# Splitting x of batch 0 by pair of heads, and the first f pair's products by pair, in an attention and FFN kernel

## The chip, the cores and the metric

The kernel runs on one core of a Trainium2 chip. Its time is the device time in microseconds (us) of one execution. The engines are PE (matrix products; PEld is its loading of weights), DVE (vector), ACT (scalar and activations), POOL (GpSimd) and SP, which issues the transfers. Each engine works through its own queue in order, and semaphores make it wait for results of the others.

## The reference

Eight batches of eight heads, 576 positions, 64 values to a head. Each head gets two attentions, one over positions averaged by fours and repeated, one over a band of seven neighbours; their sum, laid out as 4608 tokens of 512 values, goes through a feed-forward network (FFN) with 2048 hidden values.

```python
out_up = np.repeat(sm_attn(q_d, k_d, v_d), 4, axis=2)      # q_d, k_d, v_d: means over 4 positions
mask = np.abs(pos[:, None] - pos[None, :]) < 4
scores = np.where(mask, scale * np.matmul(q, k.transpose(0, 1, 3, 2)), -1000000000.0)
...
x = np.ascontiguousarray(attn_out.transpose(0, 2, 1, 3)).reshape(B * S, H * D)
h = x @ w_in
r = np.maximum(h, 0.0)
g = s * (r * r) + b
return (g @ w_out).astype(np.float32)
```

w_in and w_out come as 64-bit floats, as pairs of 32-bit words.

## The kernel before

**The work.** A batch's attention is done for four pairs of heads (HP = 4; pair `hp` is heads 2hp and 2hp+1, 128 partitions of values). The result of a batch is `x`, with 128 partitions, four pairs and 576 positions. The FFN goes over 18 blocks of 256 tokens (`t`) and 8 f pairs of 256 hidden values (`p`). Blocks 0 and 1 are the first 512 tokens, all of batch 0; block 2 has its last 64 and the first 192 of batch 1.

**Products of 32-bit accuracy.** x, the hidden values and the weights are each split into a high part, rounded to the fp32r format, and a low part, the difference. Each product is made of three: high by high, low by high, high by low. `split_x` (L517) makes `xh` by a cast on ACT (L530) and `xl` by a subtraction on DVE (L531), for all four pairs of a block at a time. `convert` (L213) turns the 64-bit weights into such halves: ACT L225, DVE L226 to L229, ACT L230 for the high part, POOL L233 for the low one. `split_w(p)` (L235) does this for f pair p.

**The FFN.** `gemm1(t, p)` (L539) makes 24 products of 128x256 into a PSUM bank `ph`: for both halves j of the f pair, for each pair of heads k, the three of L544 to L546. Then ACT applies relu (L554), squares (L555) and casts to `gh` (L556), and DVE makes `gl` (L557). `gemm2(t, p)` multiplies with w_out (L582 to L584) and sums over p; it follows gemm1 two steps later. The order of the steps is a list: blocks 0 and 1 in turn over the first seven f pairs, then block 2, then the rest.

**Batch 0's attention.** `first_unit(0, hp, ...)` (L333) makes one pair: pooled scores (L297) and softmax, the band's scores (L377), softmax (L382 to L390), transposes (L315, L317, L400), copies into block-diagonal form (L403), products with v (L326, L328, L420), and at last two additions on DVE (L423), each of which writes 288 positions of x. POOL adds up v (L282 to L287) and scales the band's weights (L390). Pair 0 has tiles of its own, pairs 1 to 3 borrow memory that later holds weights (`flat` in the trace). Batches 1 and 2 use the same function, their steps spread among the FFN's.

**What sets the order.** A scheduler places each instruction in its engine's queue by priority, in the order of the program unless a block says otherwise, when its own simulation of the kernel finds its inputs ready. Batch 0's pairs stand under `tc.high_priority(offset=400)`, batch 1's under 300; the weights of some f pairs are put back by an offset (BEHIND). In the program the border between attention and FFN is:

```python
        with tc.high_priority(offset=400):
            for _ in first_unit(0, hp, bk):
                pass
    split_w(0)
    load_w(1)
    load_w(2)
    split_x(0)
    split_x(1)
```

Batch 0's attention takes PSUM banks 0 to 3 and 5 to 7 in turn; gemm1 of block 0 uses bank 4, that of block 1 bank 7 (for p below 7). `xh` and `xl` have two buffers each.

Of the kernel before, what the change touches and what calls it, by code (L numbers as in the profile page):

```python
# [10 lines left out]
F32 = mybir.dt.float32  # L11
F32R = mybir.dt.float32r
# [3 lines left out]
ALU = mybir.AluOpType  # L16
AX = mybir.AxisListType

P = 128
B, H, S, D = 8, 8, 576, 64  # L20
HP = H // 2
# [14 lines left out]
TB = 256  # L36
NB = NT // TB
NFP = DFF // 256
NK = DM // P
# [22 lines left out]
def attention_ffn_kernel(ctx, tc, qk, vw_in, vr_in, vdm, qkn, vn, w_in, w_out, s_in, b_in, out):  # L62
    nc = tc.nc
# [4 lines left out]
    two = ctx.enter_context(tc.tile_pool(name="two", bufs=2))  # L68
    ps = ctx.enter_context(tc.tile_pool(name="ps", bufs=1, space=PS))

    def bank(i, shape, name):
        return ps.tile(shape, F32, tag=f"k{i}", name=name)
# [109 lines left out]
    def clear(i):  # L182
        da, vm = room[i]["dg"], room[i]["sc"][:, 1536:1792]
        n = 2 * NG * P
        for j in range(0, n + QV, 488):
            nc.gpsimd.memset(da[:, j : min(j + 488, n + QV)], 0.0)
        nc.gpsimd.memset(vm, 0.0)
        diag[i] = (take(da, 0, [P, 2 * NG, P]), *blocks(da, n, vm))


    wi, wo, wst = {}, {}, {}
# [4 lines left out]
    def load_w(p):  # L196

        parts = (("i", src_i[:, :, 512 * p : 512 * p + 512]), ("o", src_o[:, 2 * p : 2 * p + 2]))
        for op, src in parts:
            st = one.tile([P, 1024, 2], I32, tag=f"w{op}{STAGE[p]}", name="wst")  # L200
            nc.sync.dma_start(st.rearrange("p (k f) t -> p k (f t)", k=src.shape[1]), src)
            wst[(p, op)] = st
# [32 lines left out]
    def split_w(p):  # L235
        with tc.high_priority(offset=-BEHIND.get(p, 0)):
            split_parts(p)

    def split_parts(p):
        wi[p] = one.tile([P, 2, NK, 256], F32R, tag=f"wi{p}", name="wi")  # L240
        wo[p] = one.tile([P, 2, 2, DM], F32R, tag=f"wo{p}", name="wo")
        for op, w in (("i", wi[p]), ("o", wo[p])):
            fl = w.rearrange("p s k f -> p s (k f)")
            if p < len(STAGE):
                st = wst.pop((p, op))
                for j in range(0, 1024, CHUNK[p]):
                    js = slice(j, j + CHUNK[p])
                    convert(st[:, js], fl[:, 0, js], fl[:, 1, js], op, p)
            else:
                for i in range(4):  # L250
                    cs = slice(256 * i, 256 * i + 256)
                    convert(load_quarter(p, op, i), fl[:, 0, cs], fl[:, 1, cs], op, p)


    xt = {}
# [259 lines left out]
    xs = {}  # L515

    def split_x(t):  # L517
        tags = ("os", "xl2") if t == 2 else ("xh", "xl")
        pool = one if t == 2 else two
        xh = pool.tile([P, HP, TB], F32R, tag=tags[0], name="xh")  # L520
        xl = pool.tile([P, HP, TB], F32R, tag=tags[1], name="xl")
        t0 = t * TB
        while t0 < (t + 1) * TB:
            b = t0 // S
            while (b, HP - 1) not in complete:
                next(gen)
            n = min((t + 1) * TB, (b + 1) * S) - t0
            src = xt[b][:, :, t0 - b * S : t0 - b * S + n]
            dst = slice(t0 - t * TB, t0 - t * TB + n)
            nc.scalar.copy(xh[:, :, dst], src)  # L530
            nc.vector.tensor_tensor(  # L531
                xl[:, :, dst], src, xh[:, :, dst].bitcast(F32), ALU.subtract)
            t0 += n
        xs[t] = (xh, xl)

    gt = {}
    oacc = {}

    def gemm1(t, p):  # L539
        xh, xl = xs[t]  # L540
        ph = bank(6 if t >= 3 and p % 2 else 7 if t == 1 and p < HF else 4, [P, 2, TB], "ph")
        for j, k in itertools.product(range(2), range(NK)):
            f = slice(P * j, P * j + P)
            nc.tensor.matmul(ph[:, j], wi[p][:, 0, k, f], xh[:, k], start=(k == 0), stop=False)  # L544
            nc.tensor.matmul(ph[:, j], wi[p][:, 0, k, f], xl[:, k], start=False, stop=False)  # L545
            nc.tensor.matmul(ph[:, j], wi[p][:, 1, k, f], xh[:, k], start=False, stop=(k == NK - 1))  # L546
        if t >= 3 and p % 3 == 2:
            both = one.tile([P, 2, 2, TB], F32R, tag="xl2", name="gb")
            gh, gl = both[:, 0], both[:, 1]
        else:  # L550
            gh = two.tile([P, 2, TB], F32R, tag="gh", name="gh")
            gl = two.tile([P, 2, TB], F32R, tag="gl", name="gl")
        with tc.high_priority():
            nc.scalar.activation(ph, ph, AF.Relu)  # L554
            nc.scalar.activation(ph, ph, AF.Square)  # L555
            nc.scalar.copy(gh, ph)  # L556
            nc.vector.tensor_tensor(gl, ph, gh.bitcast(F32), ALU.subtract)  # L557
        gt[(t, p)] = (gh, gl)
# [47 lines left out]
    def load_ahead(i):  # L606
        for j in range(i, min(i + 3, EU)):
            load_pair(*units[j])
# [11 lines left out]
    for hp in range(HP):  # L620
        load_ahead(hp)
        if hp > 1:
            clear(hp)
        with tc.high_priority(offset=400):
            for _ in first_unit(0, hp, bk):
                pass
    split_w(0)
    load_w(1)
    load_w(2)
    split_x(0)  # L630
    split_x(1)


    order = [(t, p) for p in range(HF) for t in range(2)]
# [37 lines left out]
    for st, (t, p) in enumerate(order):  # L672
        gemm1(t, p)
        if st in at_step:
            split_w(at_step[st])
            if at_step[st] + 2 < len(STAGE):
                load_w(at_step[st] + 2)
        advance(st + 0.5)
        pend.append((t, p))
        if len(pend) > (2 if t < 3 else 3):  # L680
            gemm2(*pend.pop(0))
        advance(st + 1)
        if (t, p) in splits:
            split_x(splits[t, p])
# [64 lines left out]
```

## Time and profile before

| what | value |
|---|---|
| three runs | 993.43, 995.52, 996.3 us; median 995.52 |
| profiled execution, its own time | 995.95 us |
| its span | 994.2 us |
| PE busy | 957.1 us (96%) |
| PEld busy | 853.8 us |
| DVE, ACT, POOL busy | 620.4, 476.6, 467.1 us |
| mean granted clock of PE | 0.976 |

Busy time is the time in which an engine has an instruction running. The granted clock is the share of PE's full speed. A row of a time line gives start and length in us, the engine, the line of the code, the operation, and the tiles as output<-inputs; neighbouring rows of one line are drawn together with their count, and a bracket at the end gives the idle time before the row and what ended it. PE's rows overlap, so the distance of two starts is what a product takes of PE's time.

### The profile page before, as it was taken

What the parts mean: (1) busy time and instruction counts of PE and PEld (TensorE: products, weight loads), DVE (VectorE), ACT (ScalarE), POOL (GpSimd) and SP (SyncE); (2) the same over time, 40 slices, a digit from 0 to 9 for tenths busy, and PEclk for the clock granted to TensorE, in tenths of its full rate; (3) what the DMA queues carried; (4) which work ended last, traced back from release to release, by engine and by line L of the source; (5) the groups of instructions that cost most, each with busy time, mean ns of one, the idle gap of its engine ahead of it and who ended that gap; (6) DMA issues with size and microseconds to landing.
All of it is one profiled execution on the core that took longest, in us unless ns stands there. A gap on an engine that the chain in (4) does not pass through costs nothing.

```text
span 994.2 us, 18568 instructions
## 1 busy us (share of the span) xinstructions
PE 957.1 (96%) x7346; PEld 853.8 (86%) x7346; DVE 620.4 (62%) x1108; ACT 476.6 (48%) x1141; POOL 467.1 (47%) x491
## 2 busy tenths in 40 slices
PE   5769899999999999999999999999999999999998
PEld 4558788788898989898999899989898999999997
DVE  5899985322447688877778887586878772211111
ACT  4867675433465444443456344454546453333231
POOL 9544552000027668676676777474777660000000
PEclk9659999999999999999999999999999999999999
DMA  9728413111231323231333133131323110000000
GB/s 313 251 79 274 137 40 96 36 50 33 88 117 62 114 79 121 87 101 63 97 100 134 64 103 100 37 134 45 128 72 122 63 42 1 23 1 22 1 22 22
DMA packets 32103, 86.27 MB, mean 87 GB/s; under 512 B 3344, under 2 KB 7952, under 8 KB 32016
## 3 DMA queue, kind: packets, MB, share of 16 engines
q1 hardware_dynamic: 32016, 85.08, 26.0%
q8 instruction: 58, 0.95, 0.4%
q14 instruction: 29, 0.24, 0.1%
HBM read 75.63 MB, written 9.44 MB: 86 GB/s over the span
## 4 chain that ended last, share of the span: by engine, by line
PE 71%; DVE 9%; DMA 8%; POOL 5%; ACT 4%; issue 3%; SPq 1%; DVEq 0%; POOLq 0%; ACTq 0%
PE ph L544 11%; PE ph L546 11%; PE ph L545 11%; PE po L582 11%; PE po L583 10%; PE po L584 10%; DMA wst<-in_moe_w_out_dram 3%; DMA tqk<-in_qk_dram 2%; POOL pr L455 2%; PE sa L297 2%; PE up L328 1%; DVE es L229 1%; DVE es L228 1%; DMA wst<-in_moe_w_in_dram 1%; POOL acc L477 1%
## 5 line engine op out<-in xcount | busy, mean ns | idle before, releaser
L544 PE MATMUL ph<-xh,wi 128*128 128x256 f32 x1152 | 328.4, 285 | 2.8 <-ACT xh L530 2.1
L545 PE MATMUL ph<-xl,wi 128*128 128x256 f32 x1152 | 325.4, 283 | 3.4 <-DVE xl L531 3.4
L546 PE MATMUL ph<-xh,wi 128*128 128x256 f32 x1152 | 325.9, 283 | 0.0
L455 POOL TENSOR_TENSOR pr<-lqk 128x576 f32<-128x576 f32 x140 | 202.3, 1467 | 87.9 <-DMA lqk<-in_qkn_dram 71.7
L544 PEld LDWEIGHTS ph<-xh,wi 128*128 128x128 f32 x1152 | 218.4, 190 | 9.7 <-ACT xh L530 2.4
L545 PEld LDWEIGHTS ph<-xl,wi 128*128 128x128 f32 x1152 | 218.4, 190 | 8.5 <-DVE xl L531 3.7
L546 PEld LDWEIGHTS ph<-xh,wi 128*128 128x128 f32 x1152 | 218.8, 190 | 0.8
L554 ACT ACTIVATE ph<-ph 128x512 f32<-128x512 f32 x144 | 83.7, 581 | 248.4 <-PE ph L546 248.3
L582 PE MATMUL po<-wo,gh 128*128 128x512 f32 x456 | 183.8, 403 | 3.1 <-ACT gh L556 2.9
L583 PE MATMUL po<-wo,gh 128*128 128x512 f32 x456 | 182.9, 401 | 0.0
L584 PE MATMUL po<-wo,gl 128*128 128x512 f32 x456 | 180.2, 401 | 0.0
L557 DVE TENSOR_TENSOR gl<-ph,gh 128x512 fp32r<-128x512 f32 x114 | 78.1, 685 | 129.5 <-ACT gh L556 127.5
L477 POOL TENSOR_TENSOR acc<-acc,pv 128x576 f32<-128x576 f32 x80 | 115.2, 1440 | 67.4 <-DVE acc L477 38.3
L457 DVE TENSOR_REDUCE st<-pr 128x9 f32<-128x576 f32 x140 | 106.0, 757 | 42.6 <-POOL pr L455 40.2
L582 PEld LDWEIGHTS po<-wo,gh 128*128 128x128 f32 x456 | 86.2, 189 | 19.3 <-ACT gh L556 4.2
L584 PEld LDWEIGHTS po<-wo,gl 128*128 128x128 f32 x456 | 86.4, 190 | 17.5
L583 PEld LDWEIGHTS po<-wo,gh 128*128 128x128 f32 x456 | 86.4, 189 | 15.9
L556 ACT CAST gh<-ph 128x512 fp32r<-128x512 f32 x114 | 66.6, 584 | 65.2 <-PE po L583 64.0
L476 DVE TENSOR_TENSOR pv<-lv,st 128x576 f32<-128x576 f32 x120 | 87.4, 748 | 16.8 <-POOL acc L477 16.2
L555 ACT ACTIVATE ph<-ph 128x512 f32<-128x512 f32 x144 | 83.7, 582 | 3.2
L287 POOL TENSOR_TENSOR dq<-vq 64x64 f32<-64x64 f32 x58 | 21.7, 373 | 112.8 <-PE up L326 110.6
L583 PE MATMUL po<-wo,gb 128*128 128x512 f32 x120 | 48.0, 400 | 0.0
(143 smaller groups left out, 1294.9 us busy)
## 6 DMA issues: line engine op xcount, KB each, us to landing
tqk<-in_qk_dram SPq DMA_DIRECT2D x30, 584.0 KB, 3.9
lqk<-in_qkn_dram SPq DMA_DIRECT2D x20, 768.0 KB, 4.2
lv<-in_vn_dram SPq DMA_DIRECT2D x20, 480.0 KB, 3.6
out_dram<-os SPq DMA_DIRECT2D x17, 512.0 KB, 3.1
wst<-in_moe_w_in_dram SPq DMA_DIRECT2D x7, 1024.0 KB, 7.9
wst<-in_moe_w_out_dram SPq DMA_DIRECT2D x7, 1024.0 KB, 5.3
tvd<-in_vdm_dram SPq DMA_DIRECT2D x29, 160.0 KB, 2.9
tvr<-in_vr_dram SPq DMA_DIRECT2D x29, 128.0 KB, 2.1
```

The costliest lines, as they stand in the source:

```text
L455: nc.gpsimd.tensor_tensor(pr, lqk[:, 0:CH], lqk[:, CH + o : 2 * CH + o], ALU.mult)
L457: nc.vector.tensor_reduce(ls[:, :, o], pr, AX.X, ALU.add)
L476: nc.vector.tensor_tensor(pv, lv[:, o : o + CH], w, ALU.mult)
L477: (nc.vector if o % 3 == 1 else nc.gpsimd).tensor_tensor(acc[:, :, h], acc[:, :, h], pv, ALU.add)
L544: nc.tensor.matmul(ph[:, j], wi[p][:, 0, k, f], xh[:, k], start=(k == 0), stop=False)
L545: nc.tensor.matmul(ph[:, j], wi[p][:, 0, k, f], xl[:, k], start=False, stop=False)
L546: nc.tensor.matmul(ph[:, j], wi[p][:, 1, k, f], xh[:, k], start=False, stop=(k == NK - 1))
L554: nc.scalar.activation(ph, ph, AF.Relu)
L555: nc.scalar.activation(ph, ph, AF.Square)
L582: nc.tensor.matmul(po[m], gh[:, j, ms], wo[p][:, 0, j], start=first, stop=False)
L583: nc.tensor.matmul(po[m], gh[:, j, ms], wo[p][:, 1, j], start=False, stop=False)
L584: nc.tensor.matmul(po[m], gl[:, j, ms], wo[p][:, 0, j], start=False, stop=last)
```

## The change

A new function `split_pair(t, hp)` splits one pair of heads of one block: a cast of 128x256 on ACT and a subtraction of 128x256 on DVE. It makes the block's two tiles when it is first called for that block. It is called for blocks 0 and 1 right behind each pair of batch 0, at that pair's priority; the calls of `split_x(0)` and `split_x(1)` behind the weights are taken away. In `gemm1(0, 0)` and `gemm1(1, 0)` the 24 products are put in the order of the pairs of heads (all of pair 0 for both halves j, then pair 1 and so on), as one accumulation over the bank: the first product starts it and the last one ends it. All other steps keep their order. The whole diff:

```diff
@@ -533,17 +533,34 @@
             t0 += n
         xs[t] = (xh, xl)
 
+    def split_pair(t, hp):
+
+        if t not in xs:
+            xs[t] = tuple(
+                two.tile([P, HP, TB], F32R, tag=tag, name=tag) for tag in ("xh", "xl"))
+        xh, xl = xs[t]
+        src = xt[0][:, hp, TB * t : TB * t + TB]
+        nc.scalar.copy(xh[:, hp], src)
+        nc.vector.tensor_tensor(xl[:, hp], src, xh[:, hp].bitcast(F32), ALU.subtract)
+
     gt = {}
     oacc = {}
 
     def gemm1(t, p):
         xh, xl = xs[t]
         ph = bank(6 if t >= 3 and p % 2 else 7 if t == 1 and p < HF else 4, [P, 2, TB], "ph")
-        for j, k in itertools.product(range(2), range(NK)):
+
+        jks = list(itertools.product(range(2), range(NK)))
+        apart = t < 2 and p == 0
+        if apart:
+            jks.sort(key=lambda jk: jk[1])
+        for i, (j, k) in enumerate(jks):
             f = slice(P * j, P * j + P)
-            nc.tensor.matmul(ph[:, j], wi[p][:, 0, k, f], xh[:, k], start=(k == 0), stop=False)
+            first = i == 0 if apart else k == 0
+            last = i == len(jks) - 1 if apart else k == NK - 1
+            nc.tensor.matmul(ph[:, j], wi[p][:, 0, k, f], xh[:, k], start=first, stop=False)
             nc.tensor.matmul(ph[:, j], wi[p][:, 0, k, f], xl[:, k], start=False, stop=False)
-            nc.tensor.matmul(ph[:, j], wi[p][:, 1, k, f], xh[:, k], start=False, stop=(k == NK - 1))
+            nc.tensor.matmul(ph[:, j], wi[p][:, 1, k, f], xh[:, k], start=False, stop=last)
         if t >= 3 and p % 3 == 2:
             both = one.tile([P, 2, 2, TB], F32R, tag="xl2", name="gb")
             gh, gl = both[:, 0], both[:, 1]
@@ -624,11 +641,11 @@
         with tc.high_priority(offset=400):
             for _ in first_unit(0, hp, bk):
                 pass
+            for t in range(2):
+                split_pair(t, hp)
     split_w(0)
     load_w(1)
     load_w(2)
-    split_x(0)
-    split_x(1)
 
 
     order = [(t, p) for p in range(HF) for t in range(2)]
```

## The prediction

> **What bounds the kernel now.** I read the page's head first, then a table of stretches, then PE's waits, then the time lines of DVE, GpSimd (POOL) and PE around the place that the change touches. The profiled execution took 995.95 us by its own time, of which the span is
>
> ```profile
> span 994.2 us, 18568 instructions
> ```
>
> so about 1.8 us lie around it. The median of the three runs is 995.52 us, 0.43 below. My sums are made on 995.95 and carried over to the median. The table of stretches gives, for each, its length, then the busy time of PE, PEld, DVE, ACT and POOL, the granted clock and the DMA share.
>
> ```profile
> 30.00:58.00 28.00, 21.03 (x340) 16.50 (x331) 23.23 (x58) 22.81 (x64) 11.76 (x12) 0.58 0.53 174
> 40.00:43.10 3.10, 0.00 (x0) 0.00 (x0) 3.10 (x11) 1.99 (x5) 1.04 (x1) 0.50 0.01 5
> 45.00:50.00 5.00, 5.00 (x82) 4.33 (x79) 4.28 (x11) 4.92 (x15) 0.89 (x1) 0.50 0.42 173
> 52.00:60.00 8.00, 5.53 (x37) 4.07 (x38) 6.31 (x16) 6.30 (x16) 2.36 (x2) 0.50 0.37 101
> 62.00:68.00 6.00, 0.58 (x1) 0.28 (x1) 6.00 (x6) 3.74 (x6) 5.85 (x9) 0.50 0.12 33
> 76.00:100.00 24.00, 23.35 (x254) 20.40 (x251) 22.99 (x38) 18.98 (x39) 11.86 (x9) 1.00 0.81 274
> 100.00:125.00 25.00, 21.88 (x230) 18.40 (x229) 23.05 (x35) 17.40 (x39) 13.88 (x12) 0.93 0.42 137
> 125.00:200.00 75.00, 72.52 (x632) 61.81 (x631) 43.03 (x86) 42.10 (x101) 22.32 (x27) 0.97 0.18 57
> ```
>
> Three things are to be seen. From 125 us on PE is busy nearly all the time (72.52 of 75), so what counts there is only when PE gets there. From 62 to 68 us PE stands nearly still (0.58 of 6.00) while DVE is full (6.00 of 6.00): this is the border between attention and the FFN, where the change lies. And from 76 to 125 us DVE is nearly full as well (22.99 of 24, then 23.05 of 25), with PE losing 3.1 us in the second of these: DVE is close behind PE there. What PE waited for from 62 to 200 us:
>
> ```profile
> PE ph L545 <- DVE xl L531: 3.4, 1, 3.4
> PE po L582 <- ACT gh L556: 2.4, 2, 2.0
> PE ph L544 <- ACT xh L530: 2.1, 1, 2.1
> PE tp L315 <- ACT pd L308: 1.6, 1, 1.6
> PE sl L372 <- ACT pd L301: 0.7, 1, 0.7
> ```
>
> The longest wait and the third are those of the first FFN products for the two splits of batch 0's x: 5.5 us together. The fourth and fifth are products of batch 1's attention that wait for the chain over DVE and ACT; the fourth is this one:
>
> ```profile
> 118.47 0.89 PE L315 MATMUL tp<-ident,pd 96*80 96x96 f32 x3 [1.65 <-ACT pd L308]
> ```
>
> Why the split takes so long is shown by DVE's time line (start, length, engine, line):
>
> ```profile
> 62.53 0.39 DVE L423 TENSOR_TENSOR x<-ol,flat 128x288 f32<-128x288 f32 x1
> 62.84 0.75 DVE L229 SCALAR_TENSOR_TENSOR es<-wst,es 128x512 int32<-128x512 int32 x1
> 63.51 4.47 DVE L531 TENSOR_TENSOR xl<-x,xh 128x1024 fp32r<-128x1024 f32 x1
> ...
> 69.84 1.21 DVE L531 TENSOR_TENSOR xl<-x,xh 128x1024 fp32r<-128x1024 f32 x1
> ```
>
> The two L531 are the same operation on the same shape, once 4.47 us and once 1.21. Beside the long one POOL ran without a hole:
>
> ```profile
> 63.12 0.65 POOL L286 TENSOR_TENSOR dq<-vt 80x64 f32<-80x64 f32 x1
> 63.73 1.26 POOL L233 TENSOR_TENSOR wo<-es,wo 128x512 fp32r<-128x512 f32 x1
> 64.95 0.45 POOL L283 TENSOR_TENSOR vq<-tvr 128x128 f32<-128x128 f32 x1
> 65.36 0.31 POOL L286 TENSOR_TENSOR dq<-vt 80x64 f32<-80x64 f32 x1
> 65.64 1.25 POOL L233 TENSOR_TENSOR wi<-es,wi 128x512 fp32r<-128x512 f32 x1
> 66.86 1.70 POOL L282 TENSOR_TENSOR vt<-tvd 80x256 f32<-80x256 f32 x1
> ```
>
> I read 4.47 - 1.21 = 3.26 us as time in which DVE was kept out by POOL. Last, PE's products of the first f pair:
>
> ```profile
> 68.42 0.41 PE L546 MATMUL ph<-xh,wi 128*128 128x256 f32 x1
> 68.63 0.41 PE L544 MATMUL ph<-xh,wi 128*128 128x256 f32 x1
> ...
> 72.97 0.28 PE L544 MATMUL ph<-xh,wi 128*128 128x256 f32 x1
> 73.09 0.28 PE L545 MATMUL ph<-xl,wi 128*128 128x256 f32 x1
> ...
> 75.32 0.28 PE L546 MATMUL ph<-xh,wi 128*128 128x256 f32 x1
> ...
> 78.58 0.39 PE L544 MATMUL ph<-xh,wi 128*128 128x256 f32 x1 [0.65 <-DVE gl L557]
> ```
>
> They start 0.21 us apart at first and 0.12 us apart once the clock is up; the 48 of both blocks end at 75.60. At 78.58 the second f pair begins.
>
> **The change part by part.** What the splits cost as they are and in pieces shows in the answers for lines 530 and 531 up to 160 us (shortest, median, longest in ns; the shortest is in both cases the one of 256 elements, in the split of block 2):
>
> ```profile
> L530 ACT CAST xh<-x x3: 398/1040/1046, 60.3 to 140.3; 128x1024 fp32r<-128x1024 f32 x2, 128x256 fp32r<-128x256 f32 x1
> L531 DVE TENSOR_TENSOR xl<-x,xh x3: 953/1214/4471, 63.5 to 142.7; 128x1024 fp32r<-128x1024 f32 x2, 128x256 fp32r<-128x256 f32 x1
> ```
>
> Removed: two casts of 128x1024 on ACT (2.09 us) and two subtractions on DVE (4.47 + 1.21 = 5.68 us), all between 60.3 and 71.1 us. Added: eight casts of 128x256, 8 x 0.40 = 3.2 us, and eight subtractions. A free piece is worth a quarter of the free 1.21, some 0.3, and I take 0.35 with its overhead; the one that was measured took 0.95. Upper bound for a blocked one: 0.35 + 3.26 = 3.6 us. No instruction moves on the SP or POOL queue and no DMA is issued by a split; the splits pass the conversion of pair 0's weights in the order of the program, and take the attention's own priority.
>
> *DVE's term.* Two of the eight pieces must follow the last pair of heads, six go ahead of it. The stretch behind the last pair loses 5.68 us and gets two pieces; POOL's train lies there, so I take the 0.95 row for each: 5.7 - 1.9 = 3.8 us. Ends: 5.7 - 0.7 = 5.0 if both are free, and 5.7 - 7.2 = -1.5 if both are blocked in full, which leaves room for a loss.
>
> *The six earlier pieces* lie between 30 and 58 us: 6 x 0.35 = 2.1 us on DVE and 6 x 0.40 = 2.4 us on ACT, in a stretch in which DVE is idle for 28 - 23.23 = 4.8 us and ACT for 28 - 22.81 = 5.2. That idle time is their cover, twice what they need; where it doesn't lie at the right place they push the last pair back, by 4.5 us at most. I take 1.0. DVE's lead behind the border is then 3.8 - 1.0 = 2.8 us.
>
> *PE's term.* The new order (by pair of heads, both halves of f) lets 36 of the 48 products run before the last pair is there. It adds none, and one product costs the same. They need the first f pair's weights, whose last low part is done at 31.86 + 2.52 = 34.4 us:
>
> ```profile
> 31.86 2.52 POOL L233 TENSOR_TENSOR wi<-es,wi 128x512 fp32r<-128x512 f32 x2
> ```
>
> PE has holes: 3.10 us at 40 to 43.1 us and 8.00 - 5.53 = 2.5 us at 52 to 60. In the first only block 0's products of the first pair will be ready for sure (6); the second takes 2.5 / 0.21, some 11. So 17 are gone by 60 us and 31 are left. With the 1.0 of delay they start at 63.0: the first 4 us at 0.21 are 19 products, the other 12 at 0.12 take 1.4: end at 68.4, against 75.6. PE's lead is 7.2 us. The last x is there before (62.92 + 1.0 + 0.40 + 0.95 = 65.3), so that wait is hidden by the products of the other pairs; if POOL's train holds the last piece up to 66.86 + 1.0, by 0.5 us it isn't.
>
> *What ends last.* PE's lead can be kept only as far as DVE and the weights follow. The weights do: the tightest is the sixth f pair, whose low part is done at 129.98 and whose first product starts at 138.69, 8.7 us later.
>
> ```profile
> 128.37 1.61 POOL L233 TENSOR_TENSOR wi<-es,wi 128x512 fp32r<-128x512 f32 x1 [4.43 <-ACT wi L230]
> ```
>
> ```profile
> 138.69 0.28 PE L544 MATMUL ph<-xh,wi 128*128 128x256 f32 x1
> ```
>
> DVE does in part: its weight conversions can be put off within that slack, but the attention chain of batch 1, at which PE already waits before 118.47 us, can't. So the gain lies between DVE's lead of 2.8 and PE's of 7.2; I take the middle, 5.0 us. 995.95 - 5.0 = 991.0 for the profiled execution, 990.5 for the median.
>
> *Two rules weighed against rows.* Row: L531 began at 63.51 while L286 was running (to 63.77), and ended at 67.98; four further POOL operations began before that, two of them L233 at their full 1.25 us. The Trainium skill, "SBUF — State Buffer", section "Who interferes with whom", says that whichever of DVE and GpSimd issues first holds the shared ports for the whole instruction and that the other blocks until it is finished. By that rule L531 would have ended near 63.77 + 1.21 = 65.0; the row is 3.0 us later, so the trace disagrees about how long the loser waits. By the rule a piece waits for one POOL operation at most (1.26), two cost at most 3.2 us, and DVE's lead is at worst 5.7 - 3.2 - 1.0 = 1.5 us.
>
> Row: from 45 to 50 us PE is busy for 5.00 of 5.00 us at a clock of 0.50. The Trainium skill, "TensorE: Matmul & The Clock Gate", section "Part 1: The HAM clock gate (the "warmup" mystery)", has the clock raised after about 3.4 us of sustained activity. The trace disagrees for these small attention products (the FFN products' own rise, 68.0 to about 72.5, fits). By the rule the 19 slow products would be 0.09 us shorter, PE's lead 8.9 and the time 989.7 instead of 990.5.
>
> **The rivals.** *All of PE's lead arrives.* The conversions give way within their slack of 8.7 us and the attention's waits move with the order of PE's queue. For it: DVE is idle for 32 of 75 us from 125 us on, so it can catch up. Against: 23.05 of 25 busy before that. 995.5 - 7.2, with some cold products fewer: 987.5, down to 985.
>
> *The lead is swallowed.* PE comes earlier and waits longer for batch 1's chain and for gl, and the clock falls in these waits (0.93 on the mean of 100 to 125 us already shows this once). For it: that DVE row. Then the gain is 0 to 2.8 us: 994.
>
> *It doesn't happen.* Priorities order the queues; the products may stay behind the attention's in PE's queue, or wait for whole tiles. Against the second: xh at 60.3 started before x's last part was written at 62.53, so parts are waited for by themselves. Then DVE's few microseconds are lost in the earlier pieces: 995.
>
> *Slower: early products block PE's queue.* PE works in order. A product of an early pair stands ahead of attention products of the later pairs, and waits for its xl piece; behind it wait L297, L377 and L420, and behind them DVE and ACT, which need those results. If such a piece meets POOL as L531 did, all lose 3.26 us (pair 0's pieces fall near the two L233 at 31.86). From three such waits it decides: 5.0 - 3 x 3.26 = -4.8, so 1000.3. Against: before 60 us POOL is idle for more than half of the time (11.76 of 28). By the skill's rule on the ports such a wait is 1.26 at most, and this rival would hardly be there; as the row speaks against the rule, I leave it its chance.
>
> **How the numbers follow.** A measurement of this kernel tells about 0.3%, 3 us, from no change. Forecast 0.44 (990.5, its own range 987.5 to 993), all of PE's lead 0.18 (987.5), swallowed 0.20 (994), doesn't happen 0.08 (995), slower 0.10 (1000.3). Faster by over 0.3% is the first two, 0.62; within 0.3% the next two, 0.28; slower 0.10. The range goes from 985 to 997.5: it leaves out the slower case (0.10) and the outermost ends of the others (together under 0.10).
>
> **What would show each step.** Right: eight L530 and L531 pieces near 0.40 and 0.35 to 0.95 us; some 17 FFN products before 60 us; the wait for L531 gone or under 1 us; the 48 products done near 68 us; the second f pair near 71; a longer wait of PE on attention (L372, L315) at 100 to 125 us, by 2 us or so. Wrong: x of the last pair more than 2 us later than 62.9; pieces of 2 us and more; PE waits on L531 before 60 us; the second f pair no earlier than 77; or a lead that is there at 125 us and gone by 200.

## The result, and the profile after

The changed kernel takes 1001.01 us (median of 6 runs, 999.64 to 1002.17) beside 995.44 us for the kernel before (6 runs, 993.43 to 997.21). The ratio is 1.0051, with a 95% interval of 1.0036 to 1.0066: slower by some 5 us. The forecast of 990.5 us had the wrong sign, and its range ended at 997.5. The profiled execution took 1000.06 us by its own time, 4.1 us more than that of before. The head of its page:

```profile
span 998.3 us, 18577 instructions
PE 955.2 (96%) x7346; PEld 851.8 (85%) x7346; DVE 627.8 (63%) x1114; ACT 479.0 (48%) x1147; POOL 467.6 (47%) x491
```

The table of stretches of the changed kernel, with the columns of the prediction's:

```profile
62.00:68.00 6.00, 2.91 (x8) 1.98 (x8) 6.00 (x8) 3.37 (x7) 4.92 (x9) 0.50 0.10 35
76.00:100.00 24.00, 23.53 (x242) 21.02 (x243) 22.50 (x33) 16.38 (x35) 11.15 (x7) 0.88 0.74 271
100.00:125.00 25.00, 23.23 (x216) 20.49 (x215) 23.00 (x33) 16.38 (x30) 15.54 (x13) 1.00 0.37 113
125.00:200.00 75.00, 69.36 (x669) 59.27 (x669) 44.89 (x93) 45.18 (x114) 21.84 (x31) 0.95 0.23 68
250.00:560.00 310.00, 306.80 (x2206) 276.01 (x2205) 227.75 (x397) 150.83 (x379) 191.23 (x185) 1.00 0.30 96
```

The last of these stretches in the kernel before:

```profile
250.00:560.00 310.00, 309.74 (x2239) 280.89 (x2237) 227.18 (x399) 150.87 (x381) 193.63 (x186) 1.00 0.29 96
```

The border (62 to 68 us) did improve: PE is busy for 2.91 us where it had 0.58. From 125 to 200 us PE loses 3.2 us against before. And from 250 to 560 us, nearly 180 us behind the last instruction that the diff touches, PE does 309.74 - 306.80 = 2.9 us less work at the same clock of 1.00. That last loss was in no step of the prediction. What PE waited for there (waits of PE, 250 to 560 us, changed kernel: total us, times, longest):

```profile
PE ph L561 <- DVE gl L574: 1.8, 3, 1.4
PE ph L561 <- DVE gb L574: 1.0, 1, 1.0
```

In the kernel before PE waits for neither in that stretch. The longest of these waits, in the time line of the changed kernel:

```profile
520.00 0.97 POOL L283 TENSOR_TENSOR vq<-tvr 128x128 f32<-128x128 f32 x1
520.57 3.55 DVE L531 TENSOR_TENSOR xl<-x,xh 128x1024 fp32r<-128x1024 f32 x1
520.93 0.73 POOL L282 TENSOR_TENSOR vt<-tvd 80x256 f32<-80x256 f32 x1
521.62 1.42 POOL L477 TENSOR_TENSOR acc<-acc,pv 128x576 f32<-128x576 f32 x1
524.04 0.68 DVE L574 TENSOR_TENSOR gl<-ph,gh 128x512 fp32r<-128x512 f32 x1
...
524.77 0.39 PE L561 MATMUL ph<-xh,wi 128*128 128x256 f32 x1 [1.37 <-DVE gl L574]
```

A later block's split stands ahead of gl in DVE's queue and meets POOL, 3.55 us where the prediction's free row has 1.21; gl is late, and PE stands for 1.37 us. The kernel before has the same split ahead of the same gl:

```profile
516.56 0.74 POOL L282 TENSOR_TENSOR vt<-tvd 80x256 f32<-80x256 f32 x1
517.84 1.21 DVE L531 TENSOR_TENSOR xl<-x,xh 128x1024 fp32r<-128x1024 f32 x1
518.06 2.29 POOL L477 TENSOR_TENSOR acc<-acc,pv 128x576 f32<-128x576 f32 x1 [0.76 <-DVE acc L477]
518.97 0.68 DVE L557 TENSOR_TENSOR gl<-ph,gh 128x512 fp32r<-128x512 f32 x1
```

So it is not the place of the split in the queue that differs here, but what POOL does when it starts. Before, POOL stands still then (L282 was over 0.54 us earlier); its next operation, L477, starts 0.22 us behind the split and is the one that takes longer (2.29 us, 1.42 in the rows above). With the change L283 is still running when the split starts, and the split ends behind three POOL operations. Ahead of this place the queues do differ. In the traces they are those of before again from 463 us on; up to there neighbours are exchanged (behind 250 us mostly gl, gb or a reduction a few places earlier or later on DVE, one operation on POOL, three transfers on SP). The scheduler orders every queue by its own simulation, so a changed beginning can move ties long behind it. How these exchanges add up to the shift at 520 us was not followed step by step.

### The profile page after: what moved, and what is told of

Read it like the earlier page. It is cut to its first block, busy times and chain, and to the rows that moved or that the text cites. A ratio compares the mean times of both kernels' runs of the same rounds, so it can differ in the third digit from the quotient of the medians.

```text
span 998.3 us, 18577 instructions
## 1 busy us (share of the span) xinstructions
PE 955.2 (96%) x7346; PEld 851.8 (85%) x7346; DVE 627.8 (63%) x1114; ACT 479.0 (48%) x1147; POOL 467.6 (47%) x491
## 4 chain that ended last, share of the span: by engine, by line
PE 61%; DVE 13%; POOL 12%; DMA 7%; issue 5%; ACT 3%; SPq 0%; POOLq 0%; DVEq 0%; ACTq 0%
PE ph L561 9%; PE ph L562 9%; PE ph L563 9%; PE po L599 9%; PE po L600 9%; PE po L601 9%; POOL pr L455 4%; POOL acc L477 3%; DMA lqk<-in_qkn_dram 2%; DMA tqk<-in_qk_dram 2%; DVE es L228 1%; DVE es L229 1%; DMA wst<-in_moe_w_out_dram 1%; PE sa L297 1%; DVE st L457 1%
## 5 line engine op out<-in xcount | busy, mean ns | idle before, releaser
L477 POOL TENSOR_TENSOR acc<-acc,pv 128x576 f32<-128x576 f32 x80 | 114.5, 1431 | 67.8 <-DVE acc L477 36.8
```

The costliest lines, as they stand in the source:

```text
L477: (nc.vector if o % 3 == 1 else nc.gpsimd).tensor_tensor(acc[:, :, h], acc[:, :, h], pv, ALU.add)
```

## The experiments

Two theories stood at first. T1: the border costs next to nothing, and the loss lies in the later order of the queues. T2: the loss is made at the border (late x of the last pair, late chain of batch 1), and what follows only carries it. All ratios are to the kernel before, with the 95% interval; the kernel before had 995.58 to 995.96 us beside them.

**A barrier ahead of the step (4, 0)**, in both kernels, is reached at about 305 us and lets all engines start from there together.

```diff
     for st, (t, p) in enumerate(order):
+        if (t, p) == (4, 0):
+            tc.strict_bb_all_engine_barrier()
         gemm1(t, p)
```

> The kernel before with a barrier of all engines ahead of step (4, 0), near 305 us, so that the queues behind it stand in one order whatever went before. Both theories expect it a few us above 995.4, say 998 to 1006, for emptying and refilling the engines; it is only the base for the next run.

> The changed kernel with the same barrier; behind it the queues are in the same order as in bar_before. Theory 1 (the border between attention and FFN gains some 3 us that is used up by 210 us, and the 4 to 5 us are lost between 210 and 560 us, where the queues' order differs far from the change): within 1.5 us of bar_before. Theory 2 (all is lost at the border, by the later last pair and the low clock): 4 to 6 us above bar_before.

Measured: 1005.52 us (1.0096, 1.0082 to 1.0111) without the change and 1006.14 (1.0109, 1.0095 to 1.0122) with it. The barrier itself costs 10 us; with it on both sides the change costs 0.6 us, inside the intervals. That speaks for T1: what is done up to 305 us can be had with the changed border at about the same time. In both, the split near 520 us takes 1.22 us.

**One part alone.** order_only keeps the old splits and only orders the first products; pieces_only splits by pair and keeps the old order of the products.

```diff
-            for t in range(2):
-                split_pair(t, hp)
...
+    split_x(0)
+    split_x(1)
```

> The whole-block splits as before, only the first f pair's products by pair of heads. Both theories: the products wait for the whole split, nothing changes, 995.4 within 1.5 us.

```diff
-        apart = t < 2 and p == 0
+        apart = False
```

> The splits in pieces as in the change, the first f pair's products in the old order. Theory 1: the queues fall back into the order of the kernel before by some 250 us, so no later loss; the border alone decides, and with 9 instead of 18 products of each block free of the last pair it gains little or nothing: 994 to 998. Theory 2: the last pair is as late as in the change and fewer products are done ahead, 18 x 0.12 to 0.21 us more: 1003 to 1005.

Measured: 995.38 us (0.9999, 0.9986 to 1.0011) and 998.64 us (1.0032, 1.0017 to 1.0047). The queues of order_only are those of before, line by line: without pieces no product can start earlier, and its ratio shows how well no change is measured. The pieces alone cost 3.2 us, although pieces_only has the queues of before from 240 us on and no PE idle time from 250 to 560 us. So something can be lost at the beginning too.

**The same border, another later order.** Batch 2's attention stands under a priority of 60. With 50 the changed kernel keeps its own order up to 199 us and has that of the kernel before from 240 us on; the kernel before, with 50, keeps its own order up to 181 us and has that of the changed kernel from 250 us on.

```diff
-            with tc.high_priority(offset=300 if done < NY[1] else 60 if done < NY[1] + NY[2] else 0):
+            with tc.high_priority(offset=300 if done < NY[1] else 50 if done < NY[1] + NY[2] else 0):
```

> The changed kernel with the priority of batch 2's attention lowered by a hair (offset 50 for 60). By the program as it is built, all queues stand as in the changed kernel up to about 200 us, and from about 230 us on as in the kernel before: the change's border with the old later order. Theory 1 (the loss is in the later order): 994 to 997.5. Theory 2 (the loss is at the border): 1000 to 1002.

> The kernel before with the same hair (offset 50 for 60). Its queues stand as before up to about 200 us and from about 240 us on as in the changed kernel: the old border with the later order of the change. Theory 1: slower than the kernel before by 3 to 5 us, 998.5 to 1000.5. Theory 2: within 1.5 us of 995.5.

Measured: after_offset50 995.17 us (0.9996, 0.9985 to 1.0008); before_offset50 994.0 us (0.998, 0.997 to 0.9991). The first refutes T2: the whole change at the border, and no loss. Since it shares all queues with the changed kernel up to 199 us, the 0.55% between the two are made behind that. The second refutes T1 in its simple form, that the later order is bad by itself: the kernel before gains 2 us with it.

**When and where the pieces are made.** late_pieces leaves only those of the last pair at the attention's priority and puts the others behind pair 0's weights in the program (in the trace, three of those six xl pieces still start by 54 us); pool_pieces makes the subtractions on POOL; last_first orders the first products from the last pair backwards, so that no product is early.

```diff
-            for t in range(2):
-                split_pair(t, hp)
+            if hp == HP - 1:
+                for t in range(2):
+                    split_pair(t, hp)
     split_w(0)
+    for hp in range(HP - 1):
+        for t in range(2):
+            split_pair(t, hp)
```

> As the change, but the pieces of pairs 0 to 2 at the natural priority behind pair 0's weights; only the last pair's pieces keep the attention's priority. From about 220 us on its queues stand as in the kernel before. If the pieces on DVE and ACT push the last pair back (by 3.2 us in the change), its x comes within 1 us of 62.9 again and the first f pair's products end at 69 to 71: 993 to 996. Rival, that the early products in PE's queue push it back: x stays near 65.7, 996 to 998.

```diff
-        nc.vector.tensor_tensor(xl[:, hp], src, xh[:, hp].bitcast(F32), ALU.subtract)
+        nc.gpsimd.tensor_tensor(xl[:, hp], src, xh[:, hp].bitcast(F32), ALU.subtract)
```

> As the change, but the eight xl pieces are made by GpSimd instead of DVE. From about 210 us on its queues stand as in the kernel before. If DVE's queue is what holds the pieces and the last pair back, the last pair's x comes at 63 to 64.5, the last xl piece within 2 us of it instead of 3, and the time is 993 to 996. Rival, that GpSimd's own train of operations holds the last piece: last xl piece at 68 or later, 996 to 998.

```diff
-            jks.sort(key=lambda jk: jk[1])
+            jks.sort(key=lambda jk: -jk[1])
```

> The eight pieces as in the change, but the first f pair's products in the opposite order, the last pair of heads first, so that no product can run ahead of it. From about 220 us on the queues stand as in the kernel before. If the pieces themselves (on DVE and ACT) make the last pair late, its x comes at 65 to 66 as in the change. If the early products in PE's queue do it, its x comes at 62.5 to 63.5. Time: 997 to 1000 in the first case, 995 to 997 in the second; there are no early products to gain from in either.

Measured: 996.19 us (1.0002, 0.9985 to 1.0019), 997.59 us (1.0025, 1.0013 to 1.0037) and 994.99 us (0.9994, 0.9981 to 1.0007). All three have the later order of before. Without early products, and with the pieces, last_first is even with the kernel before, as after_offset50 is with all of them: early products bring nothing. pieces_only, with the same pieces and 18 early products, is 3.8 us slower than last_first by the ratios; why is not shown. Taking the subtractions from DVE (pool_pieces) doesn't help: 0.25% slower. The last pair's x (the start of the second L423) is at 64.98 us in late_pieces and at 65.24 in pool_pieces, and pool_pieces has its last xl piece at 69.32, so both times the rival holds; in last_first x is at 63.96, between the two cases.

**Fewer pieces, and the priority once more.** three_and_one splits three pairs at once behind the third and the last pair alone; three_and_one_o50 has the priority of 50 as well; after_offset100 is the changed kernel with 100 for the 60.

```diff
-            for t in range(2):
-                split_pair(t, hp)
+            if hp >= HP - 2:
+                for t in range(2):
+                    split_pairs(t, 0 if hp == HP - 2 else hp, hp + 1)
```

> As the change, but pairs 0 to 2 split at once (128x768, one cast and one subtraction a block) when pair 2 is done, then the last pair: four of each operation instead of eight, none in the stretch of GpSimd's first weight lows. From about 210 us on the queues stand as in the kernel before. If single pieces held by GpSimd and their number make the last pair late, its x comes within 1.5 us of 62.9 and the time is 993 to 995.5. If any work put there does, x is at 65 again and the time 996 to 998.

> three_and_one with offset 50 for 60: its queues fall into the changed kernel's later order from about 240 us on. If that later order is bad by itself, 3 to 5 us above three_and_one. If it is only bad with the change's border, whose batch 1 is late (x of batch 1 at 172.5 against 164), it is 1 to 3 us below three_and_one, as before_offset50 was below the kernel before.

```diff
-            with tc.high_priority(offset=300 if done < NY[1] else 60 if done < NY[1] + NY[2] else 0):
+            with tc.high_priority(offset=300 if done < NY[1] else 100 if done < NY[1] + NY[2] else 0):
```

> The changed kernel with offset 100 for 60: all queues as in the changed kernel but for a handful of swaps between about 160 and 240 us, then the changed kernel's later order to the end. In three runs that later order showed 2 to 4 us of PE waiting for gl and gb between 250 and 560 us, with the other order at most 0.3. If that is the change's loss, these waits are here again and the time is 998 to 1001. If the loss hung on chances of the stretch around 200 us, which is swapped here, the time is 994 to 997 with the waits there or not.

Measured: 1001.5 us (1.0052, 1.004 to 1.0064), 999.09 us (1.0032, 1.002 to 1.0044) and 997.24 us (1.0014, 1.0001 to 1.0027). three_and_one is as slow as the change, with the later order of before; its time is lost ahead of that order. Its last x is at 65.31 us, the case "any work put there", but its time lies 3.5 us above that case. The two others have the later order of the changed kernel: three_and_one_o50 is 2.4 us below three_and_one, the second of its cases, and after_offset100 has the waits again but stays below the 998 us that they were to bring.

**What the runs add up to.** Call the later order of the kernel before A, that of the changed kernel B. PE's waits from 250 to 560 us in the three other kernels with B are before_offset50:

```profile
PE ph L544 <- DVE gl L557: 1.4, 1, 1.4
PE ph L544 <- DVE gb L557: 0.6, 1, 0.6
```

after_offset100:

```profile
PE ph L561 <- DVE gl L574: 2.0, 3, 1.5
PE ph L561 <- DVE gb L574: 0.6, 1, 0.6
```

and three_and_one_o50:

```profile
PE ph L561 <- DVE gl L574: 2.5, 3, 1.3
PE ph L561 <- DVE gb L574: 1.4, 1, 1.4
```

after_offset50 and three_and_one, both with A, have none. The split near 520 us takes 3.55 us in all four kernels with B, where POOL's L283 runs when it starts, and 1.21 or 1.22 us in the ten others, where POOL stands still then. In the table, "at the end" is the ratio less 1 times 995.5 us. "250 to 560" is PE's idle time there, from the profile, less the 0.26 us of before; the clock is 1.00 there in all of them, and from 560 us on PE is busy in each but for at most 0.2 us until the last 4 us of the program. The last column is the difference of the two: what must have come by 250 us. "At the end" carries some 1.0 to 1.5 us of uncertainty, and "by 250 us" at least as much, as its other term is one execution's.

| kernel | border | later order | at the end | 250 to 560 | by 250 us |
|---|---|---|---|---|---|
| changed kernel | pieces by pair | B | +5.1 | +2.9 | +2.2 |
| after_offset50 | pieces by pair | A | -0.4 | -0.3 | -0.1 |
| after_offset100 | pieces by pair | B | +1.4 | +2.5 | -1.1 |
| before_offset50 | as before | B | -2.0 | +1.8 | -3.8 |
| three_and_one | three and one | A | +5.2 | -0.3 | +5.5 |
| three_and_one_o50 | three and one | B | +3.2 | +3.9 | -0.7 |

Two things are shown. B costs 1.8 to 3.9 us between 250 and 560 us, in all four kernels that have it, by waits for gl and gb; A costs nothing there. And the changed border is neutral when A follows it (-0.4 us, and 0.6 with the barriers). A third is read off with less certainty: with two of the borders B is 3.8 us (-3.8 to the 0 of the kernel before) and 6.2 us (+5.5 to -0.7) better by 250 us, which more than pays for the waits behind; with the changed border it isn't, at 60 (+2.3 against A), and is within the uncertainty at 100 (-1.0). So the change loses 2.9 us to the waits of B. The 2.2 us ahead of them are less sure: the two profiled executions are 4.1 us apart, which leaves 1.2. And the stretch up to 250 us isn't alike in two executions: the granted clock from 125 to 250 us is 0.97 in the changed kernel and 1.00 in bar_after, though the two have the same queues up to 281 us, and 0.03 of 125 us are nearly 4 us. What makes the stretch from 176 to 247 us, where the queues with 60 and with 100 differ, go worse with 60 stays open.

The fastest kernel of all leaves the border alone: before_offset50, one number changed, 994.0 us.

## Why the prediction was wrong

**The step that failed is "What ends last".** It took the gain to lie between DVE's lead of 2.8 and PE's of 7.2 us, and 5.0 in the middle. At the border the runs showed no gain in place of the 5.0 us (after_offset50, -0.4 us with 1.2 of uncertainty either way). DVE's lead was nil. PE's was 2.1 us at the second f pair, and while step (0, 4) still started 3.0 us earlier than before (122.04 for 125.08), step (2, 0), which needs batch 1's x, started 8.3 us later (175.88 for 167.56): the prediction's sign "a lead that is there at 125 us and gone by 200". And the order of the queues, which the prediction took as fixed behind the border ("No instruction moves on the SP or POOL queue"), changed up to 463 us; on POOL the L233 of wo now stands at 63.73 us ahead of the L286 that it followed.

**The six earlier pieces: 1.0 us of delay taken, 3.2 measured.** The additions that write x (the view of line 423, 57 to 175 us: count, shortest, median and longest in ns, first and last start), before:

```profile
L423 DVE TENSOR_TENSOR x<-ol,ups x8: 441/444/452, 79.5 to 164.2; 128x288 f32<-128x288 f32 x8
L423 DVE TENSOR_TENSOR x<-ol,flat x2: 390/420/451, 59.6 to 62.5; 128x288 f32<-128x288 f32 x2
```

and with the change:

```profile
L423 DVE TENSOR_TENSOR x<-ol,ups x8: 442/448/453, 84.2 to 172.9; 128x288 f32<-128x288 f32 x8
L423 DVE TENSOR_TENSOR x<-ol,flat x2: 445/446/447, 62.8 to 65.7; 128x288 f32<-128x288 f32 x2
```

The last pair's x (second row of each) is 65.7 - 62.5 = 3.2 us later, which the prediction had named as a sign of being wrong (over 2). In last_first, with the pieces and no early products, the same two start at 60.75 and 63.96, 1.2 and 1.4 us later. The clock of the attention doesn't explain this: four kernels with the queues of before have this x at 62.5 to 63.0 us, while their clock from 0 to 62 us goes from 0.78 to 0.94. By this one pair of kernels about 1.3 us are the pieces' and 1.8 the early products', which stand in PE's queue ahead of the last pairs' attention. The sum isn't that simple, though: with 18 early products pieces_only has its x at 63.79 and late_pieces at 64.98. Early products in the way are the mechanism of the rival "slower", at some 1.8 us instead of three times 3.26; it alone didn't make the kernel slower, as after_offset50 shows.

**DVE's term: 2.8 us taken, nothing measured.** The pieces have the size that was taken:

```profile
L544 DVE TENSOR_TENSOR xl<-x,xh 128x256 fp32r<-128x256 f32 x8 | 4.6, 579 | 0.0
```

Eight of them take 4.6 us in place of 5.68. What failed is where the last two stand. DVE's time line of the changed kernel:

```profile
62.83 0.45 DVE L423 TENSOR_TENSOR x<-ol,flat 128x288 f32<-128x288 f32 x1
63.19 0.54 DVE L387 TENSOR_REDUCE sm<-pl 128x12 f32<-128x384 f32 x1
63.65 0.68 DVE L229 SCALAR_TENSOR_TENSOR es<-wst,es 128x512 int32<-128x512 int32 x1
64.25 1.49 DVE L227 TENSOR_SCALAR es<-es 128x512 int32<-128x512 int32 x1
65.66 0.45 DVE L423 TENSOR_TENSOR x<-ol,flat 128x288 f32<-128x288 f32 x1
66.03 2.09 DVE L226 TENSOR_SCALAR es<-es 128x512 f32<-128x512 f32 x1
68.03 0.69 DVE L388 TENSOR_SCALAR sm<-sm 128x12 f32<-128x12 f32 x1
68.64 0.41 DVE L544 TENSOR_TENSOR xl<-x,xh 128x256 fp32r<-128x256 f32 x1
...
70.05 0.36 DVE L544 TENSOR_TENSOR xl<-x,xh 128x256 fp32r<-128x256 f32 x1
```

The weights' conversions (L226 to L229) and the softmax of the next pair (L387, L388) stand in the gap that the pieces were to leave. The piece of block 0 starts at 68.64, though its x was there at 63.28 and its cast at 63.7, and the old xl of block 0 was done at 67.98: the blocking by POOL went over to L227 (1.49) and L226 (2.09). The same two operations on the same shape take 0.41 and 0.42 at 69.58 and 70.92 us, so 1.08 + 1.67 = 2.75 us are lost there, beside a POOL that runs without a hole from 63.73 to 68.69 us, against 3.26 in the old xl. The stall left the split and came back at its neighbours in the full queue.

**PE's term: 17 early products taken, 36 measured; a lead of 7.2 us taken, 2.1 measured.** All products of pairs 0 to 2 had started by 55.0 us. They came so early because PE found more holes than the two that were counted, and because from 50 us on they ran 0.12 us apart, not the 0.21 taken: the clock from 30 to 58 us was 0.93, where the profile of before had 0.58. But the last twelve wait for the last pair. PE's time line of the changed kernel:

```profile
66.59 0.58 PE L561 MATMUL ph<-xh,wi 128*128 128x256 f32 x1 [2.25 <-ACT xh L543]
69.11 0.58 PE L562 MATMUL ph<-xl,wi 128*128 128x256 f32 x1 [1.93 <-DVE xl L544]
...
71.48 0.41 PE L563 MATMUL ph<-xh,wi 128*128 128x256 f32 x1
...
73.80 0.80 PE L599 MATMUL po<-wo,gh 128*128 128x512 f32 x1 [1.91 <-ACT gh L573]
...
76.47 0.58 PE L561 MATMUL ph<-xh,wi 128*128 128x256 f32 x1 [0.59 <-DVE gl L574]
76.85 0.42 PE L562 MATMUL ph<-xl,wi 128*128 128x256 f32 x1
77.06 0.42 PE L563 MATMUL ph<-xh,wi 128*128 128x256 f32 x1
...
81.12 0.41 PE L561 MATMUL ph<-xh,wi 128*128 128x256 f32 x1
```

The 48 end at 71.9 us (taken: 68.4; before: 75.6). The waits for xh and xl fell from 5.5 to 2.25 + 1.93 = 4.2 us; that they would nearly go was wrong, since the last pair's x was 3.2 us late and its two xl pieces started 5.4 and 3.9 us behind the end of their x. The second f pair starts at 76.47, 2.1 us earlier than before, where 71 was taken. Its products then run 0.21 us apart, where before they ran at 0.12: the long run of products within which the clock rose at 72 us before is cut up now, and the clock rises at 81.6 us (81.2 to 81.6 in the four kernels with this border, 71.5 to 74.0 in the four with the old one). 22 products at 0.09 us more are 2.0 us, nearly the whole lead. The prediction counted cold products on the first f pair alone; less work left there means that the next pair meets the cold clock.

**Behind the border.** Batch 1's x comes 4.7 us (84.2 to 79.5) to 8.7 us (172.9 to 164.2) later, and PE's idle time from 125 to 200 us rises from 2.5 to 5.6 us. Part of this was foreseen as the rival "the lead is swallowed": 0 to 2.8 us of gain, and after_offset50 (-0.4 us) is in that range. That rival, at 994 us and 0.20, describes what the change does at its own place. What the prediction did not have at all is that the same edit picks another order up to 463 us, and that this is worth more than the edit.

**The rule on the ports.** The first piece started at 33.41 us and took 1.87 us, where the seven others together take 2.76. POOL's row beside it:

```profile
32.50 2.51 POOL L233 TENSOR_TENSOR wi<-es,wi 128x512 fp32r<-128x512 f32 x2
```

The piece ended at 35.28, just behind the second of these two POOL operations, not behind the first. By the rule of the Trainium skill, "SBUF — State Buffer", section "Who interferes with whom", it would have waited for one; the trace disagrees again, as it did at 63.51 us before (where five further POOL operations began before the split ended, not the four that the prediction counted).

## What to carry to other kernels

Where a scheduler orders the queues, an edit at one place is also a new draw of the order everywhere behind it: compare the queues and the start of each step over the whole run, not only at the edit, look at what each engine meets at the time and not only at its order, and separate the two with a control, such as a barrier in both kernels or a priority changed by a hair. Here kernels with one and the same border lay between 0.9996 and 1.0051. A stall removed from an engine whose queue is full can come back at the next instruction in that queue, so ask what stands behind it before counting the gain for the one that waits. And work taken out of a cold stretch of PE shortens it only as far as what follows doesn't become cold in its stead (here 22 products, 2.0 us).

## What the runs showed of the hardware

That a priority of 50 or 60 for one batch's attention moves the time of the kernel before by 2 us, at equal work, was not expected. Neither was the size of POOL's hold on DVE: 3.55 us for an operation that takes 1.21 us free, far from the border, and 2.09 us for an L226 of 128x512 whose next one takes 0.42 (at 66.03 and 70.92 us of the changed kernel). Nor that it hangs on which of the two starts first, at the same places in the queues: near 520 us POOL's L283 had begun 0.57 us ahead of the split in the kernels with 3.55 us, and in those with 1.21 us POOL's next operation began 0.22 us behind it and was the longer one (2.29 us). The granted clock of a stretch is no property of the queues: with the same ones it was 0.97 and 1.00 from 125 to 250 us, and 0.78 to 0.94 up to 62 us.
